# Keys and values in lasting buffers with zeroed rows, and pairs of heads taken two by two

## The chip, the cores and the metric

The kernel runs on one core of a Trainium2 chip. The metric is the device time of one execution in microseconds (us). TensorE (PE in the profile, its weight loads PEld) multiplies into the accumulation memory (PSUM), VectorE (DVE) and ScalarE (ACT) do element by element work, GpSimd (POOL) helps them, and SyncE (SP) issues most DMA transfers.

## What is computed

A linear attention over 8 batches, 8 heads, 576 positions and 64 columns, then two feed-forward layers over the 4608 rows that come out.

```python
q_s = exp(q - max(q, axis=-1)); q_s = q_s / (sum(q_s, axis=-1) + 1e-9)
k_s = exp(k - max(k, axis=2));  k_s = k_s / (sum(k_s, axis=2) + 1e-9)
kv = einsum('bhsd,bhse->bhde', k_s, v)          # 64x64 for each head
x = einsum('bhsd,bhde->bhse', q_s, kv)          # -> 4608 x 512
x = maximum(x @ w_in, 0) ** 2 @ w_out           # 512 -> 2048 -> 512
xn = x / sqrt(mean(x * x) + 1e-6) * rms_g
out = (silu(xn @ w_gate) * (xn @ w_val)) @ w_out2   # 512 -> 1536 -> 512
```

## The kernel before

The 4608 rows are taken in 9 blocks of 512 (`NB`). The first feed-forward layer runs block by block in 16 units each (`FF1`): in a unit (j, c), `p1_A` makes twelve products into `ps_h` (four 128-row pieces, three passes each over high and low halves of the numbers), ScalarE and VectorE turn them into `g` (`p1_hi`, `p1_lo`), and `p1_B` adds twelve products into `acc`, two units later. Weights come from DRAM through a ring of seven tiles `ws` (`RING`, `feed`), eight of them stay. The second layer follows from block 8 on in an order of its own (`plan2`).

Attention of block j is worked out while block j-1 is in the first layer, for blocks 0 and 1 ahead of everything (`ROUND`, lines 1150 to 1172). It goes by pairs of heads hp (four of them, `NP`), so that a pair fills 128 columns. From block 2 on each step of a pair has a place in `HALVES` (lines 1084 to 1088), counted in half units, slots: `attention(2 * i)` runs after the ps_h products of unit i, `attention(2 * i + 1)` at its end, after the acc products. Pairs are eight slots apart, line 1093 sets the start. The order of instructions on each engine is that of the program (`pinned`, `InOrder`), so a step that waits holds what is behind it on its engine.

The steps of one pair: `a_loadk`, `a_loadq`, `a_loadv` load; `a_kmax` (VectorE: `mk`), `a_kt` (TensorE transposes it into `ps_kt`), `a_mc` (VectorE: `mc`, `mcb`) and `a_kb` (TensorE: `ps_kb`) find the greatest key of each column; `a_ksub` (VectorE) and `a_kexp` (ScalarE, into `ke`) make the exponentials; `a_qmax`, `a_qsub`, `a_qexp`, `a_qsum`, `a_qn` make those of q, and `a_qT` (four transposes into `ps_q`), `a_qT_hi`, `a_qT_lo` turn them. `a_kv` multiplies `ke` by `vt` into `ps_kv`: the 576 positions are five chunks, four of 128 rows and one of 64 (`SR`), for two heads, whose results lie in the partitions 0 to 63 and 64 to 127. `vt` has a 65th column of ones, which gives the sum of the keys. Each of these products is two instructions in the trace, so a pair has 20. `a_kvf` divides (VectorE), `a_kvd_hi` and `a_kvd_lo` split the result into high and low halves, `a_x` (TensorE: `ps_x`) multiplies by q, and `a_x_hi`, `a_x_lo` (ScalarE, VectorE) write the layer's input `x`.

All steps from block 2 on that need PSUM share two banks, `a0` and `a1`, which `a_ps` hands out in turn (lines 105 to 107); a step that takes a bank waits for the last reader of the step two before it.

Beside that, `tick` converts weights (`d_load` to `d_lo`, tiles `raw`, `s`, `n`, `t`) on all three engines; from block 2 on it comes in about 11 of 20 units, and `d_out` splits the results (`so`) on ScalarE and GpSimd. At the third unit of a block `p1_out` moves the block's `acc` to `e` and to DRAM.

`a_tile` (line 394) hands out the working tiles of a pair; `A_BUFS` has how many buffers each name has in the lasting pool and, for blocks 0 and 1, more in a pool that is closed later.

Of the kernel before, what the change touches and what calls it, by code (L numbers as in the profile page):

```python
# [8 lines left out]
F32 = mybir.dt.float32  # L9
F32R = mybir.dt.float32r  # L10
# [3 lines left out]
AF = mybir.ActivationFunctionType  # L14
ALU = mybir.AluOpType
# [25 lines left out]
def attention_moe_kernel(  # L41
# [14 lines left out]
    ve, se, ge, te = (  # L56
        InOrder(tc, engine, pinned) for engine in (nc.vector, nc.scalar, nc.gpsimd, nc.tensor)
    )
    B, H, S, D = q.shape
    NT, DM = out.shape  # L60
    P = 128
# [4 lines left out]
    NP = H // 2  # L66
    FF1 = w_in.shape[0]
    FF2 = w_out2.shape[0]
    SF = S // P
    SR = S - SF * P  # L70
    OFF = S - T

    const = ctx.enter_context(tc.tile_pool(name="const", bufs=1))
# [11 lines left out]
    eps_sb = const.tile([P, 1], F32, name="eps_sb")  # L85
    g_sb = const.tile([P, KD], F32, name="g_sb")
    kvd = [
        [const.tile([P, 2, P], F32R, name=f"kvd{i}_{hp}") for hp in range(NP)] for i in range(2)
    ]
    mask = const.tile([P, 2, D], F32, name="mask")  # L90
    x2d = [tc.dram_tile([P, KD, T], F32, name=f"x2d{j}") for j in range(NB)]
# [2 lines left out]
    def held(j, ins):  # L94
        return tc.keep_in_program_order(ins) if j > 0 and not pinned[0] else ins
# [9 lines left out]
    def a_ps(j, hp, name):  # L105
        turns["a"] += 1
        return ps_a.tile([P, 512], F32, tag=f"a{turns['a'] % 2}", name=name)

    def mm3(ps, lhsT, rhs, first, last, j=0, part=False):
        for n, (a, b) in enumerate(PASSES):  # L110
            ins = te.matmul(
                ps,
                lhsT(a),
                rhs(b),
                start=first and n == 0,
                stop=last and n == 2,
                skip_group_check=part,
            )
            if n == 0:
                held(j, ins)  # L120
# [56 lines left out]
    pools = {}  # L177
# [210 lines left out]
    kts, kes, vts, qts, qns, mks, mcs, qTs, qms, kvs = ({} for _ in range(10))  # L388
    xts = {}


    A_BUFS = {"kt": (3, 1), "qt": (3, 1), "vt": (2, 2), "qn": (2, 0), "ke": (1, 1), "qT": (1, 0)}

    def a_tile(j, hp, shape, tag, dtype=F32):

        n, more = A_BUFS[tag]
        at = (j * NP + hp) % (n + more) if j < 2 else 0
        if at < n:
            return pools["a"].tile([P, *shape], dtype, tag=tag, name=tag, bufs=n)
        return pools["s"].tile([P, *shape], dtype, tag=f"{tag}{at}", name=f"{tag}s", bufs=1)  # L400
# [4 lines left out]
    def hs_(hp):  # L405
        return slice(2 * hp, 2 * hp + 2)

    def a_loadk(j, hp):
        if j >= B:
            return  # L410
        kt = kts[j, hp] = a_tile(j, hp, [2, SF + 1, D], "kt")
        if j < 2:
            nc.sync.dma_start(
                out=s_chunks(kt),
                in_=k[j, hs_(hp), 0 : SF * P, :].rearrange("h (p c) d -> p c h d", c=SF),
            )
            return
        nc.sync.dma_start(
            out=kt[:, :, 0:SF, :],
            in_=k[j, hs_(hp), 0 : SF * P, :].rearrange("h (p c) d -> p h c d", c=SF),  # L420
        )
        nc.sync.dma_start(
            out=kt[0:SR, :, SF, :], in_=k[j, hs_(hp), SF * P : S, :].rearrange("h p d -> p h d")
        )

    def a_loadq(j, hp):
# [12 lines left out]
            )  # L439
        qts[j, hp] = qt  # L440

    def a_loadv(j, hp):
        if j >= B:
            return
        hs = slice(2 * hp, 2 * hp + 2)
        vt = a_tile(j, hp, [SF + 1, 2, D + 1], "vt")
        ge.memset(vt[:, :, :, D : D + 1], 1.0)
        for h in range(2):
            nc.sync.dma_start(
                out=vt[:, 0:SF, h, 0:D],  # L450
                in_=v[j, 2 * hp + h, 0 : SF * P, :].rearrange("(p c) d -> p c d", c=SF),
            )
        nc.sync.dma_start(
            out=vt[0:SR, SF, :, 0:D], in_=v[j, hs, SF * P : S, :].rearrange("h p d -> p h d")
        )
        vts[j, hp] = vt
# [61 lines left out]
    def a_kexp(j, hp):  # L518
        if j >= B:
            return  # L520
        kt = kts.pop((j, hp))
        ke = a_tile(j, hp, [SF + 1, 2, D], "ke")
        kv_ = kt.rearrange("p h c d -> p c h d")
        for rows, cs in k_parts:
            ins = se.activation(out=ke[rows, cs], in_=kv_[rows, cs], func=AF.Exp)
            held(j, ins)
        kes[j, hp] = ke
# [48 lines left out]
    def split_hi(parts, key, dst):  # L576
        src = parts[key]
        se.activation(out=dst[:, 0], in_=src, func=AF.Copy)
        parts[key] = dst, src
# [12 lines left out]
    def a_kv(j, hp):  # L592
        if j >= B:
            return
        ps = a_ps(j, hp, "ps_kv") if j > 1 else kvs.pop((j, hp))
        ke, vt = kes.pop((j, hp)), vts.pop((j, hp))
        for c in range(SF + 1):
            m = P if c < SF else SR
            for h in range(2):
                ins = te.matmul(  # L600
                    ps[h * D : (h + 1) * D, 0 : D + 1],
                    ke[0:m, c, h, :],
                    vt[0:m, c, h, :],
                    start=c == 0,
                    stop=c == SF,
                )
                if c == 0 and h == 0:
                    held(j, ins)
        kvs[j, hp] = ps

    def a_kvd_hi(j, hp):
        if j < B:
            split_hi(kvs, (j, hp), kvd[j % 2][hp])

    def a_kvd_lo(j, hp):
        if j < B:
# [3 lines left out]
    def a_kvf(j, hp):  # L620
        if j >= B:
            return
        ps = kvs.pop((j, hp))
        rk = pools["a"].tile([P, 1], F32, tag="rk", name="rk")
        ve.tensor_scalar_add(out=rk, in0=ps[:, D : D + 1], scalar1=1e-9)
        ve.reciprocal(out=rk, in_=rk)

        if j < 2:
            f = pools["sk"[j]].tile([P, P], F32, tag=f"kvf{hp}", name="kvf", bufs=1)
        else:  # L630
            f = pools["a"].tile([P, P], F32, tag="kvf", name="kvf")
        ve.scalar_tensor_tensor(
            out=f.rearrange("p (h d) -> p h d", h=2),
            in0=ps[:, 0:D].unsqueeze(1).to_broadcast([P, 2, D]),
            scalar=rk,
            in1=mask,
            op0=ALU.mult,
            op1=ALU.mult,
        )
        kvs[j, hp] = f  # L640
# [10 lines left out]
    def s_chunks(kt):  # L651
        t = kt.rearrange("p h c d -> p (h c d)")[:, 0 : 2 * SF * D]
        return t.rearrange("p (c h d) -> p c h d", c=SF, h=2)
# [52 lines left out]
        te.transpose(ps[0:SR, P : 2 * P], ek[:, SF * P : S], ident)  # L706

    def s_kc(j, hp):
        ke = kes[j, hp] = a_tile(j, hp, [SF + 1, 2, D], "ke")
        se.activation(  # L710
            out=ke[:, 0:SF].rearrange("p c h d -> p (c h d)"), in_=kT.pop((j, hp)), func=AF.Copy
        )
        ve.tensor_copy(
            out=ke[0:SR, SF].rearrange("p h d -> p (h d)"), in_=kvs[j, hp][0:SR, P : 2 * P]
        )
# [33 lines left out]
    def a_x(j, hp):  # L749
        ps = a_ps(j, hp, "ps_x")  # L750
        qT = qTs.pop((j, hp))
        p0 = min(j * OFF // NG, P)
        view = ps.rearrange("p (c t) -> p c t", c=NG)
        for b, lo, hi in ((j - 1, 0, p0), (j, p0, P)):
            if lo == hi:
                continue
            t = kvd[b % 2][hp]
            mm3(
                view[:, :, lo:hi],
                lambda a: t[:, a, :],  # L760
                lambda a: qT[:, a, :].rearrange("p (c t) -> p c t", c=NG)[:, :, lo:hi],
                True,
                True,
                j,
            )
        xts[j, hp] = ps
# [314 lines left out]
        return min(NJ1 + 4 + len(at) * 11 // 20, len(jobs) + 4)  # L1081


    HALVES = ((-12, a_loadk), (-10, a_loadq), (-3, a_kmax), (-2, a_qmax), (0, a_qsub))
    HALVES += ((0, a_loadv), (2, a_qexp), (3, a_kt), (3, a_qsum), (4, a_mc), (4, a_qn))
    HALVES += ((6, a_kb), (7, a_ksub), (8, a_kexp), (8, a_qT), (9, a_qT_hi), (10, a_qT_lo))
    HALVES += ((10, a_kv), (11, a_kvf), (12, a_kvd_hi), (13, a_kvd_lo), (14, a_x))
    HALVES += ((15, a_x_hi), (16, a_x_lo))
    todo = {}
    for j in range(2, NB):  # L1090
        for hp in range(NP):
            for n, (at, f) in enumerate(HALVES):
                at += (j - 1) * 2 * FF1 - (9 if j == 2 else 11) + 2 * FF1 // NP * hp
                todo.setdefault(at, []).append((-n, j, hp, f))
    for l in todo.values():
        l.sort(key=lambda x: x[:3])
# [19 lines left out]
    with ExitStack() as ctx_a:  # L1116
# [8 lines left out]
        def at_(f, r):  # L1125
            if 0 <= r < len(heads):
                f(*heads[r])

        a_loadk(0, 0)
        make_identity(nc, ident)  # L1130
        ge.tensor_scalar(
            out=neg_r, in0=ident, scalar1=-1.0, scalar2=0.0, op0=ALU.mult, op1=ALU.add
# [98 lines left out]
        for i, (j, c) in enumerate(units):  # L1231
# [54 lines left out]
            s = i - (n1 - FF1)  # L1286
# [6 lines left out]
        at = 0  # L1293
        for op in plan2:
# [4 lines left out]
            else:  # L1299
                _, s, n, q = op  # L1300
# [49 lines left out]
```

## Time and profile before

| | us |
|---|---|
| median of three runs | 1737.18 |
| lowest and highest run | 1733.74, 1738.27 |
| profiled execution, its time | 1733.5 |
| profiled execution, its span | 1731.5 |
| TensorE busy, matmuls | 1707.3 |
| VectorE busy | 1059.1 |
| ScalarE busy | 763.4 |

The span is the time from the first to the last instruction that the profile shows. Matmuls overlap in the records (one of 512 columns is shown with 0.39 us, though the next starts sooner), so what a group costs is read from the starts. A group on the timeline is a run of like instructions, and x20 is how many. All attention work of blocks 2 to 8 lies between about 130 and 760 us.

### The profile page before, as it was taken

To read this page: it belongs to the slowest core of one execution; us is meant where nothing else is said; L and a number is where in the kernel's file an instruction comes from. 1 tells how busy PE (TensorE), PEld (TensorE's weight loads), DVE (VectorE), ACT (ScalarE), POOL (GpSimd) and SP (SyncE) were. 2 spreads that over 40 slices of the span, in tenths; PEclk is the share of its full clock that TensorE was granted. 3 is DMA by queue.
4 is the path that set the end of the run, shared out by engine and by line. 5 is a ranking of instruction groups with operands and counts; after the bars stand their busy time and mean duration, and the time that the engine had idled before them with its cause. 6 is when DMAs were issued, how large, how long until landed. Compare 5 with 4: busy or idle time off the path is not lost.

```text
span 1731.5 us, 23049 instructions
## 1 busy us (share of the span) xinstructions
PE 1707.3 (99%) x8390; PEld 1410.3 (81%) x8390; DVE 1059.1 (61%) x1847; ACT 763.4 (44%) x1336; POOL 151.8 (9%) x167
## 2 busy tenths in 40 slices
PE   6999999999999999999999999999999999999998
PEld 5788888788888878888888888888888888888997
DVE  7996555565565556431566787757765776646344
ACT  6875445545555554443544325332523243223122
POOL 2000001223333223220000000000000000000000
PEclk9999999999999999999999999999999999999999
DMA  9986657788888877576465557566756666665885
GB/s 213 317 285 246 201 174 229 227 292 278 275 281 258 285 246 248 177 254 208 158 204 196 195 191 268 186 219 194 267 192 211 196 232 203 219 192 193 289 304 202
DMA packets 190560, 398.42 MB, mean 230 GB/s; under 512 B 65520, under 2 KB 102384, under 8 KB 189296
## 3 DMA queue, kind: packets, MB, share of 16 engines
q1 hardware_dynamic: 162416, 356.05, 64.0%
q10 hardware_dynamic: 28032, 40.90, 6.7%
q8 instruction: 67, 1.10, 0.3%
q14 instruction: 45, 0.37, 0.1%
HBM read 337.12 MB, written 59.77 MB: 229 GB/s over the span
## 4 chain that ended last, share of the span: by engine, by line
PE 95%; DVE 2%; ACT 1%; SPq 0%; DMA 0%; issue 0%; POOL 0%; DVEq 0%; POOLq 0%; ACTq 0%
PE acc L34 39%; PE ps_h L34 22%; PE ps_x L34 10%; PE ps_y L34 9%; PE ps_v L34 8%; PE ps_w L34 4%; PE ps_kv L34 1%; DVE t L34 1%; PE ps_q L34 1%; PE ps_kb L34 0%; PE ps_kt L34 0%; DVE qs L34 0%; PE ps_s L34 0%; DMA qt<-in_q 0%; DMA vt<-in_v 0%
## 5 line engine op out<-in xcount | busy, mean ns | idle before, releaser
L34 PE MATMUL ps_h<-x,ws 128*128 128x512 f32 x1296 | 316.6, 394 | 0.7 <-ACT r L34 0.7
L34 PE MATMUL acc<-ws,g 128*128 128x512 f32 x1296 | 313.4, 390 | 1.0 <-ACT g L34 0.9
L34 PE MATMUL acc<-g,ws 128*128 128x512 f32 x1296 | 313.8, 391 | 0.0
L34 PEld LDWEIGHTS acc<-ws,g 128*128 128x128 f32 x1296 | 241.4, 188 | 51.3 <-ACT g L34 2.1
L34 PEld LDWEIGHTS acc<-g,ws 128*128 128x128 f32 x1296 | 241.7, 188 | 50.9
L34 PEld LDWEIGHTS ps_h<-x,ws 128*128 128x128 f32 x1296 | 239.6, 188 | 50.8 <-ACT r L34 1.5
L34 ACT ACTIVATE g<-r 128x512 fp32r<-128x512 f32 x252 | 159.1, 631 | 230.5 <-DVE r L34 225.4
L34 DVE TENSOR_TENSOR g<-r,g 128x512 fp32r<-128x512 f32 x252 | 172.6, 685 | 116.9 <-ACT g L34 115.2
L34 ACT ACTIVATE r<-ps_h 128x512 f32<-128x512 f32 x144 | 85.7, 595 | 232.7 <-PE ps_h L34 232.6
L34 PE MATMUL ps_y<-xo,ws 128*128 128x512 f32 (+1 forms) x720 | 168.6, 369 | 0.0
L34 PE MATMUL ps_v<-xo,ws 128*128 128x512 f32 (+1 forms) x720 | 168.4, 368 | 0.0
L34 PE MATMUL ps_x<-xo,ws 128*128 128x512 f32 (+1 forms) x720 | 167.4, 368 | 0.0
L34 PEld LDWEIGHTS ps_x<-xo,ws 128*128 128x128 f32 x720 | 128.0, 188 | 23.5
L34 PEld LDWEIGHTS ps_v<-xo,ws 128*128 128x128 f32 x720 | 127.7, 188 | 23.4
L34 PEld LDWEIGHTS ps_y<-xo,ws 128*128 128x128 f32 x720 | 126.4, 189 | 24.2 <-DVE sa L34 1.5
L34 PE MATMUL ps_h<-x,w 128*128 128x512 f32 x432 | 106.1, 395 | 0.0
L34 PE MATMUL acc<-g,w 128*128 128x512 f32 x432 | 104.4, 391 | 0.0
L34 PEld LDWEIGHTS acc<-g,w 128*128 128x128 f32 x432 | 80.7, 188 | 16.9
L34 PEld LDWEIGHTS ps_h<-x,w 128*128 128x128 f32 x432 | 79.7, 188 | 17.0 <-issue 0.4
L34 ACT ACTIVATE r<-r 128x512 f32<-128x512 f32 x144 | 91.0, 632 | 4.5
L34 DVE TENSOR_TENSOR u<-ps_y,p 128x512 f32<-128x512 f32 (+1 forms) x120 | 76.0, 633 | 22.9 <-PE ps_y L34 21.5
L34 ACT ACTIVATE sg<-silu 128x512 f32<-128x512 f32 (+1 forms) x90 | 51.5, 585 | 82.4 <-DVE silu L34 82.3
(138 smaller groups left out, 1823.4 us busy)
## 6 DMA issues: line engine op xcount, KB each, us to landing
ws<-wd_t SPq DMA_DIRECT2D x210, 512.0 KB, 4.2
ws<-wd_u SPq DMA_DIRECT2D x108, 512.0 KB, 4.2
ws<-wd_o SPq DMA_DIRECT2D x96, 512.0 KB, 4.4
ws<-wd_i SPq DMA_DIRECT2D x89, 512.0 KB, 4.4
wd_t<-so ACTq DMA_DIRECT2D x84, 256.0 KB, 4.7
raw<-in_w_out SPq DMA_DIRECT2D x28, 512.0 KB, 5.2
raw<-in_w_gv SPq DMA_DIRECT2D x24, 512.0 KB, 5.6
x2d<-e SPq DMA_DIRECT2D x36, 256.0 KB, 3.0
```

Source lines behind the costliest of these rows:

```text
L34: ins = f(*args, **kw)
```

## The change

- Keys (`ke`) and values (`vt`) of blocks get lasting buffers (`kbuf`, `vbuf`), made once at the start by `a_bufs`: rows 64 to 127 of the fifth chunk are set to zero and the column of ones to one, by GpSimd. Loads and exponentials never write those rows again. The memset at each load of v is gone.
- `a_kv` uses all 128 rows in the fifth chunk too.
- From block 2 on two pairs of heads share a plan of 16 slots: `FIRST` for the even pair, `SECOND` for the odd one. `a_kv` of both stands in slot 9 and writes two halves of one PSUM bank; `a_kvf2`, `a_kvd2_hi` and `a_kvd2_lo` then work on both. The start is 4 slots ahead of the block's instead of 11 (9 for block 2).
- `kvd` tiles hold two pairs each; `kt` and `qt` have two buffers in the lasting pool instead of three.

```diff
-        [const.tile([P, 2, P], F32R, name=f"kvd{i}_{hp}") for hp in range(NP)] for i in range(2)
+        [const.tile([P, 2, 2, P], F32R, name=f"kvd{i}_{n}") for n in range(NP // 2)]
+        for i in range(2)
...
-    A_BUFS = {"kt": (3, 1), "qt": (3, 1), "vt": (2, 2), "qn": (2, 0), "ke": (1, 1), "qT": (1, 0)}
+    A_BUFS = {"kt": (2, 2), "qt": (2, 2), "qn": (2, 0), "qT": (1, 0)}
...
+    kbuf, vbuf = [], []
+
+    def a_bufs(pool, n, bufs, name, shape):
+
+        for at in range(n):
+            t = pool.tile([P, *shape], F32, tag=f"{name}{len(bufs)}", name=name, bufs=1)
+            ge.memset(t[SR:P, SF], 0.0)
+            if shape[-1] > D:
+                ge.memset(t[:, :, :, D : D + 1], 1.0)
+            bufs.append(t)
...
-        vt = a_tile(j, hp, [SF + 1, 2, D + 1], "vt")
-        ge.memset(vt[:, :, :, D : D + 1], 1.0)
+        vt = vbuf[(j * NP + hp) % (4 if j < 2 else 2)]
...
-        ke = a_tile(j, hp, [SF + 1, 2, D], "ke")
+        ke = kbuf[hp % 2]
...
-        ps = a_ps(j, hp, "ps_kv") if j > 1 else kvs.pop((j, hp))
+        if j < 2:
+            ps, o = kvs.pop((j, hp)), 0
+        else:
+            if hp % 2 == 0:
+                kvs[j, hp // 2] = a_ps(j, hp, "ps_kv")
+            ps, o = kvs[j, hp // 2], hp % 2 * P
...
-            m = P if c < SF else SR
             for h in range(2):
                 ins = te.matmul(
-                    ps[h * D : (h + 1) * D, 0 : D + 1],
-                    ke[0:m, c, h, :],
-                    vt[0:m, c, h, :],
+                    ps[h * D : (h + 1) * D, o : o + D + 1],
+                    ke[:, c, h, :],
+                    vt[:, c, h, :],
...
+    def a_kvf2(j, hp):
...
+        ps = kvs.pop((j, hp // 2))[:, 0 : 2 * P].rearrange("p (n d) -> p n d", n=2)
+        rk = pools["a"].tile([P, 2], F32, tag="rk", name="rk")
+        ve.tensor_scalar_add(out=rk, in0=ps[:, :, D], scalar1=1e-9)
+        ve.reciprocal(out=rk, in_=rk)
+        f = pools["a"].tile([P, 2, P], F32, tag="kvf", name="kvf", bufs=1)
+        for n in range(2):
+            ve.scalar_tensor_tensor(
...
-    HALVES = ((-12, a_loadk), (-10, a_loadq), (-3, a_kmax), (-2, a_qmax), (0, a_qsub))
-    HALVES += ((0, a_loadv), (2, a_qexp), (3, a_kt), (3, a_qsum), (4, a_mc), (4, a_qn))
-    HALVES += ((6, a_kb), (7, a_ksub), (8, a_kexp), (8, a_qT), (9, a_qT_hi), (10, a_qT_lo))
-    HALVES += ((10, a_kv), (11, a_kvf), (12, a_kvd_hi), (13, a_kvd_lo), (14, a_x))
-    HALVES += ((15, a_x_hi), (16, a_x_lo))
+    FIRST = ((-9, a_loadk), (-6, a_loadq), (-4, a_loadv), (0, a_kmax), (1, a_kt), (2, a_mc))
+    FIRST += ((4, a_kb), (4, a_qmax), (5, a_ksub), (5, a_qsub), (6, a_kexp), (7, a_qexp))
+    FIRST += ((8, a_qsum), (9, a_qn), (9, a_kv), (11, a_qT), (12, a_qT_hi), (13, a_qT_lo))
+    FIRST += ((14, a_x), (15, a_x_hi), (16, a_x_lo))
+    SECOND = ((-7, a_loadk), (-3, a_loadq), (-2, a_loadv), (3, a_kmax), (4, a_kt), (5, a_mc))
+    SECOND += ((6, a_kb), (7, a_qmax), (7, a_ksub), (8, a_kexp), (8, a_qsub), (9, a_qexp))
+    SECOND += ((9, a_kv), (10, a_kvf2), (11, a_qsum), (11, a_kvd2_hi), (12, a_qn))
+    SECOND += ((12, a_kvd2_lo), (13, a_qT), (15, a_qT_hi), (16, a_qT_lo), (17, a_x))
+    SECOND += ((18, a_x_hi), (19, a_x_lo))
...
-            for n, (at, f) in enumerate(HALVES):
-                at += (j - 1) * 2 * FF1 - (9 if j == 2 else 11) + 2 * FF1 // NP * hp
+            for n, (at, f) in enumerate(SECOND if hp % 2 else FIRST):
+                at += (j - 1) * 2 * FF1 - 4 + 4 * FF1 // NP * (hp // 2)
...
         a_loadk(0, 0)
+        for pool, n, bufs, name in (("a", 2, kbuf, "ke"), ("a", 2, vbuf, "vt"), ("s", 2, vbuf, "vt")):
+            a_bufs(pools[pool], n, bufs, name, [SF + 1, 2, D + (name == "vt")])
```

## Rows read from the trace of the kernel before

**Rows 1.** The page, part 1: busy us, share of the span, instructions.

```profile
PE 1707.3 (99%) x8390; PEld 1410.3 (81%) x8390; DVE 1059.1 (61%) x1847; ACT 763.4 (44%) x1336; POOL 151.8 (9%) x167
```

**Rows 2.** Busy by stretch; columns: stretch, length, engines, clock, DMA share, GB/s.

```profile
0.00:60.00 60.00, 46.07 (x349) 33.30 (x350) 49.21 (x119) 41.04 (x78) 10.39 (x30) 1.00 0.90 225
...
340.00:750.00 410.00, 405.29 (x2095) 332.18 (x2095) 235.62 (x445) 212.23 (x379) 117.63 (x109) 1.00 0.81 261
```

**Rows 3.** TensorE's waits from 130 to 900 us; columns: total us, times, longest us.

```profile
PE ps_q L34 <- DVE x L34: 4.6, 2, 3.2
```

**Rows 4.** Timeline of TensorE at one visit of products; columns: start, length (us), what.

```profile
453.19 0.39 PE L34 MATMUL acc<-g,w 128*128 128x512 f32 x1
...
453.51 0.95 PE L34 MATMUL ps_kv<-vt,ke 128*64 128x65 f32 x20
...
453.68 0.40 PE L34 MATMUL ps_kv<-vt,ke 128*64 128x65 f32 x8
...
453.91 0.29 PE L34 MATMUL ps_kv<-vt,ke 128*64 128x65 f32 x4
...
454.13 0.33 PE L34 MATMUL ps_kv<-vt,ke 64*64 64x65 f32 x4
...
454.39 0.50 PE L34 MATMUL ps_h<-x,ws 128*128 128x512 f32 x1
...
454.73 0.39 PE L34 MATMUL ps_h<-x,ws 128*128 128x512 f32 x1
```

**Rows 5.** The same timeline: ordinary products of the feed-forward layer, and four transposes.

```profile
447.98 2.88 PE L34 MATMUL acc<-g,ws 128*128 128x512 f32 x12
...
450.70 1.52 PE L34 MATMUL acc<-g,w 128*128 128x512 f32 x6
...
444.80 0.60 PE L34 MATMUL ps_q<-ident,qn 128*128 128x128 f32 x4
...
445.48 0.39 PE L34 MATMUL ps_h<-x,ws 128*128 128x512 f32 x1
```

**Rows 6.** VectorE by line, 340 to 660 us: busy us, mean ns, idle before.

```profile
L34 DVE TENSOR_REDUCE mk<-kt 128x128 f32<-128x512 f32 x13 | 14.2, 1093 | 0.0
...
L34 DVE TENSOR_TENSOR mk<-mk,kt 64x128 f32<-64x128 f32 x13 | 4.7, 362 | 0.4
...
L34 DVE TENSOR_REDUCE mc<-ps_kt 128x1 f32<-128x128 f32 x13 | 3.7, 285 | 0.7
...
L34 DVE COPY mcb<-mc 128x128 f32<-128x128 f32 x13 | 3.7, 286 | 0.4
...
L34 DVE TENSOR_TENSOR g<-r,g 128x512 fp32r<-128x512 f32 x52 | 35.0, 674 | 10.5 <-ACT g L34 10.5
...
L34 DVE TENSOR_TENSOR x<-ps_x,x 128x512 fp32r<-128x512 f32 x13 | 8.8, 679 | 0.0
...
L34 DVE SCALAR_TENSOR_TENSOR t<-s,t 128x512 uint32<-128x512 uint32 x25 | 22.5, 900 | 0.9
...
L34 DVE CUSTOM_DVE_ANT_0 t<-t,n 128x1024 uint16<-128x1024 uint16 x25 | 19.3, 771 | 0.9
...
L34 DVE TENSOR_SCALAR t<-s 128x512 uint32<-128x512 uint32 x26 | 11.9, 458 | 1.5 <-POOL so L34 1.5
```

**Rows 7.** Timeline before TensorE's longest wait; VectorE's waits (130 to 800 us).

```profile
343.16 1.70 DVE L34 SCALAR_TENSOR_TENSOR t<-s,t 128x512 uint32<-128x512 uint32 x1
...
344.89 1.64 DVE L34 CUSTOM_DVE_ANT_0 t<-t,n 128x1024 uint16<-128x1024 uint16 x1
...
347.28 0.63 PE L34 MATMUL ps_q<-ident,qn 128*128 128x128 f32 x4 [3.25 <-DVE x L34]
...
DVE t L34 <- POOL so L34: 5.0, 2, 3.6
```

**Rows 8.** Timeline: the first product; page, part 6: a ring load, us to landing.

```profile
5.36 0.66 PE L34 MATMUL ps_l<-ident,kl 64*128 64x64 f32 x4 [5.36 <-DMA kl<-in_k]
...
ws<-wd_i SPq DMA_DIRECT2D x89, 512.0 KB, 4.4
```

More of the change, by code (lines that the diff above doesn't have):

```diff
@@ L608, in a_kv, with a_kvd2_hi, a_kvd2_lo @@
                     held(j, ins)
-        kvs[j, hp] = ps
+        if j < 2:
+            kvs[j, hp] = ps
+    def a_kvf2(j, hp):
+        if j >= B:
+            return
+        ps = kvs.pop((j, hp // 2))[:, 0 : 2 * P].rearrange("p (n d) -> p n d", n=2)
[5 more added lines that the diff above has]
+            ve.scalar_tensor_tensor(
+                out=f[:, n].rearrange("p (h d) -> p h d", h=2),
+                in0=ps[:, n, 0:D].unsqueeze(1).to_broadcast([P, 2, D]),
+                scalar=rk[:, n : n + 1],
+                in1=mask,
+                op0=ALU.mult,
+                op1=ALU.mult,
+            )
+        kvs[j, hp // 2] = f
+    def a_kvd2_hi(j, hp):
+        if j < B:
+            t = kvd[j % 2][hp // 2]
+            se.activation(out=t[:, :, 0], in_=kvs[j, hp // 2], func=AF.Copy)
+    def a_kvd2_lo(j, hp):
+        if j < B:
+            t = kvd[j % 2][hp // 2]
+            ve.tensor_tensor(
+                out=t[:, :, 1],
+                in0=kvs.pop((j, hp // 2)),
+                in1=t[:, :, 0].bitcast(F32),
+                op=ALU.subtract,
+            )
     def a_kvd_hi(j, hp):
         if j < B:
-            split_hi(kvs, (j, hp), kvd[j % 2][hp])
+            split_hi(kvs, (j, hp), kvd[j % 2][hp // 2][:, hp % 2])
     def a_kvd_lo(j, hp):
@@ L623, in a_kvf @@
         ps = kvs.pop((j, hp))
-        rk = pools["a"].tile([P, 1], F32, tag="rk", name="rk")
+        rk = pools["a"].tile([P, 2], F32, tag="rk", name="rk")[:, 0:1]
         ve.tensor_scalar_add(out=rk, in0=ps[:, D : D + 1], scalar1=1e-9)
         ve.reciprocal(out=rk, in_=rk)
[L628 to L631, printed above, removed]
+        f = pools["sk"[j]].tile([P, P], F32, tag=f"kvf{hp}", name="kvf", bufs=1)
         ve.scalar_tensor_tensor(
@@ L708, in s_kc @@
     def s_kc(j, hp):
-        ke = kes[j, hp] = a_tile(j, hp, [SF + 1, 2, D], "ke")
+        ke = kes[j, hp] = kbuf[hp % 2]
         se.activation(
@@ L756, in a_x @@
                 continue
-            t = kvd[b % 2][hp]
+            t = kvd[b % 2][hp // 2][:, hp % 2]
             mm3(
```

## The prediction

> **What bounds the kernel now.** I read the page's first part, then the busy times by stretch, then TensorE's own waits, and last its timeline at single visits. TensorE is busy 99% of the span [rows 1]. After the first 60 us, where it is idle 14 us and VectorE is busy 49, it hardly stops: between 340 and 750 us it lacks 4.7 us of 410 [rows 2], and nearly all of that is one kind of wait, the transposes of q waiting for VectorE's x [rows 3]. So a microsecond less of work on TensorE's queue is a microsecond less of time, and other engines count only where TensorE waits for them. VectorE is at 57% there.
>
> A feed-forward product of 512 columns starts every 0.227 us (twelve from 447.98 to 450.70) [rows 5]. Four transposes put between two such products take 0.68 us from the first transpose to the second product after them, less one ordinary spacing 0.45, or 0.11 each [rows 5]: going from one type of work to another is free as long as both use all 128 rows and columns of the array. The visit of one pair of heads' ps_kv products, with 64 columns, is different. The product before it starts at 453.19, ps_kv at 453.51, the next feed-forward product at 454.39 and the one after that at 454.73 [rows 4]. That is 1.54 us, less two ordinary spacings 1.09 us for one visit.
>
> **What the visit consists of** [rows 4]. Five chunks of 128, 128, 128, 128 and 64 rows. From chunk 2 to chunk 4 there are 0.23 us, so 0.115 a chunk. Chunk 1 takes 0.17, so 0.055 more; the wait ahead of it is 0.32 instead of 0.227, so 0.09 more. From chunk 4 to the short one there are 0.22, 0.105 too many, and the short chunk up to the next product takes 0.26, and then the next spacing is 0.34, 0.11 too many. The reading that fits all of it: each change of the tile's shape (128x128 to 128x64, 128x64 to 64x64, 64x64 to 128x128) costs some 0.15 to 0.2 us, and there are three in a visit.
>
> **Part 1, the full-row short chunk.** It takes out the change from 128x64 to 64x64: the 0.105 and the 0.055 that chunk 5 pays on entering, 0.16 a visit. There are 24 visits in the blocks 2 to 7 (six blocks, four pairs of heads): 3.8 us. Twice the rows cost nothing where columns set the pace, as chunks 2 to 4 show. Blocks 0 and 1 have 8 more visits, at most 1.3 us, in the first 60 us, where VectorE's chain sets the pace as much as TensorE; from 0 to 1.3 I take 0.5.
>
> **Part 2, two visits in one.** In the new order both pairs' ps_kv come in the same slot with nothing of TensorE between them, into one PSUM bank. The last chunk's 0.26 less the 0.055 of its own entry is 0.205, 0.09 more than a chunk. So one entry (0.09 + 0.055) and one exit (0.09 + 0.11) are saved for two pairs: 0.345, 12 times: 4.1 us. Together, from the rows: two visits 2.17; the new double one 0.32 + 0.17 + 8 x 0.115 + 0.205 + 0.34 less 0.453, so 1.50. The difference, 0.67, carries the rounding of eight starts; with the parts above (2 x 0.16 + 0.345) it is 0.665, and from the starts to the nanosecond 0.64. I take 0.65, 12 times: 7.8 us. Bounds: 4 (one of the two parts alone) to 8.
>
> **Part 3, TensorE's waits.** A slot is half a unit: after the twelve ps_h products or after the twelve acc products; they are numbered here from the first pair's kmax, which is 0. Today the q transposes take the PSUM bank that x of the pair before held, and x_lo stands in the very slot of those transposes, behind a unit's conversion of weights on VectorE. At 347.28 TensorE had waited 3.25 us for it [rows 7]; 4.6 us in all [rows 3]. In the new order, written out with the alternation of the two banks, the transposes of q take banks whose readers are done well before: the first pair's (slot 11) that of the second ps_kb, read in slot 7; the second pair's (slot 13) that of ps_kv, read in slot 10. So these 4.6 us go, unless something new is late.
>
> What is late next? Every step now stands one to three slots behind what it needs. The tightest I find is ps_kt of the second pair in slot 4: VectorE can take mc of the first pair only when its ps_kt is out (slot 1), and has then to do mc (0.285 + 0.286), the low half of g (0.674), perhaps one conversion (0.458 + 0.900 + 0.771 = 2.13), x_lo of the pair before (0.679) and kmax (1.093 + 0.362): 3.4 us, or 5.5 with the conversion [rows 6]. TensorE in that time does three groups of twelve, 36 x 0.227 = 8.2 us. Some 2.7 us to spare, and the conversion comes in 11 units of 20 only. At slower conversions (0.41 + 1.70 + 1.64, as before the longest wait [rows 7]) it is 7.1, still in time. I take no new wait; the other end stands with the rivals.
>
> **What else moves, at nothing.** GpSimd loses the memset at each load of v (it had to wait for the last reader of its buffer) and gets ten small ones at the start; the first product waits there for a DMA until 5.36 us [rows 8], so they lie behind that wait. Loads of k, q and v go to other slots, and k and q have two buffers instead of three. SyncE issues them in order, ahead of ring loads, so a late release would hold those up. But k's buffer is asked for one slot after its exponential is issued, q's one slot after its last reader, v's three or more; and a ring load lands in 4.4 us [rows 8] with seven tiles in the ring, each lasting a group of twelve products, 2.7 us: 19 us less 4.4, so some five slots of delay are covered; past that the ring would run dry. All loads of two pairs now lie in eight of sixteen slots, with the DMA engines at 0.81 on average [rows 2]; they have nine slots or more before use. VectorE does kvf and the low half of kvd of two pairs in five instructions instead of eight, which is off the path. In block 2's steps nothing ends later than before; in later blocks the last x_lo comes two slots later, one ahead of the first product of the next block, whose tenth product needs it 2 us after.
>
> **Sum.** 7.8 + 4.6 + 0.5 = 12.9 us. The profiled execution took 1733.5 us (its span 1731.5); 1720.6 for it. It was the quickest of those shown; their median is 1737.2, so 3.7 more: 1724.3.
>
> **Rivals.**
> (a) The waits come back in another place, about as many as now: the steps stand closer, and VectorE waits for GpSimd too, 3.6 us once [rows 7]. For it: one-slot distances everywhere; against: the sum of 5.5 against 8.2. Then 7.8 + 0.5 are left: 1729.
> (b) Padding is worth nothing: the gap ahead of the short chunk is not of the shape but of the ends of its accumulation. Then 1724 + 3.8 = 1728. In its favour, from the Trainium skill (TensorE: Matmul & The Clock Gate, "Why this matters for your kernels"): a product of fewer rows lasts as long as one of 128, and short rows gain by running beside others, which this change gives up. No run here shows the two side by side; chunk 5's late start in [rows 4] speaks against it, and so does another page of the skill (TensorEngine Tiling, "Tiling Modes"), by which a change of the tiling mode empties the array.
> (c) Both at once: only the merging's 4.1 is left: 1733, no change that can be told.
> (d) Slower. VectorE misses the second ps_kt. With a slowed conversion and a 3.6 us wait for GpSimd [rows 7] ahead of it, the chain is 7.1 + 3.6 = 10.7 against 8.2: 2.5 us late. If that were so in all twelve double visits, 30 us would be added to the forecast: 1754. It decides from 12.9 / 12, or 1.1 us of lateness in each on. Against it: two such waits for GpSimd in all of 130 to 800 us. The Trainium skill (SBUF — State Buffer, "SBUF: two separate sides") gives the mechanism: VectorE with two SBUF inputs and GpSimd exclude each other for a whole instruction. The trace has 1.70 against a mean of 0.90 for one such instruction.
>
> **Chances.** Forecast 0.47; (a) 0.22; (b) 0.08; (c) 0.11; (d) 0.12. A change below 0.3%, 5.2 us, can't be told from none. Forecast, (a) and (b) are faster by more: 0.77; (c) within: 0.11; (d) slower: 0.12. The range runs from 1716 (8 for the visits, 4.6 and 1.3 make 13.9 below the profiled 1733.5, so 1720, and 4 of scatter, the distance of that run from the median) to 1735 (over (c) and its scatter); (d) and scatter are left out, about 0.2.
>
> **What would show it.** After: ps_kv in groups of 40 records with 128 rows throughout, 1.3 us from the first start to the next product and no gap between chunk 4 and 5; twelve such groups after block 1; TensorE's waits for VectorE gone between 130 and 900 us. Wrong would be: a gap at the fifth chunk with 128 rows too (b), a gap or another product between the two pairs, ps_kt, ps_kb or ps_x waiting for VectorE (a, d), or ps_h or acc waiting for a ring load.

## The result, and the profile after

The changed kernel takes 1722.85 us (median of four runs, 1722.04 to 1723.12) against 1737.06 (four runs, 1733.74 to 1738.27); the ratio is 0.992, with a 95% interval of 0.9909 to 0.9932. It is faster by 14.2 us. The profiled executions are 10.4 us apart (1733.5 and 1723.12, spans 1731.5 and 1721.3); where the other 3.8 us come from is told below.

Part 1 of the page and the busy times by stretch, of the changed kernel, answering to [rows 1] and [rows 2]:

```profile
PE 1699.7 (99%) x8390; PEld 1409.3 (82%) x8390; DVE 1064.4 (62%) x1811; ACT 758.0 (44%) x1324; POOL 151.2 (9%) x145
```

```profile
0.00:60.00 60.00, 44.44 (x343) 32.05 (x344) 47.57 (x116) 39.63 (x75) 11.30 (x31) 0.97 0.89 217
...
340.00:750.00 410.00, 410.00 (x2156) 339.64 (x2156) 243.71 (x431) 212.74 (x377) 120.26 (x97) 1.00 0.82 269
```

TensorE is busy 7.6 us less, and in the stretch from 340 to 750 us it has no idle time left (4.7 us before). The start is no shorter in this execution: TensorE's granted clock was 0.97 in the first 60 us (1.00 in the execution of [rows 2]), and the first ps_h product came 1.5 us later than there.

TensorE's waits from 130 to 900 us (total us, times, longest), answering to [rows 3]:

```profile
PE ps_kt L34 <- DVE mk L34: 0.4, 1, 0.4
```

The waits of the q transposes are gone. What stays is one of another kind: the first ps_kt of block 2 waits 0.4 us for kmax, at 153 us.

The timeline of one double visit (start us, length us, what), answering to [rows 4]. Rows cut out of a group at a later moment begin with the oldest product still running, and carry the shape of that one though the group may hold others:

```profile
488.20 0.39 PE L34 MATMUL acc<-g,w 128*128 128x512 f32 x1
...
488.52 1.39 PE L34 MATMUL ps_kv<-vt,ke 128*64 128x65 f32 x40
...
488.92 0.41 PE L34 MATMUL ps_kv<-vt,ke 128*64 128x65 f32 x8
...
489.04 0.40 PE L34 MATMUL ps_kv<-vt,ke 128*64 128x65 f32 x8
...
489.15 0.41 PE L34 MATMUL ps_kv<-vt,ke 128*64 128x65 f32 x8
...
489.83 0.50 PE L34 MATMUL ps_h<-x,ws 128*128 128x512 f32 x1
...
490.17 0.39 PE L34 MATMUL ps_h<-x,ws 128*128 128x512 f32 x1
```

All 40 products have 128 rows. The fourth chunk starts at 488.92, the fifth at 489.04, the first of the second pair at 489.15: 0.12 and 0.11 apart, with no gap ahead of the fifth chunk and none between the pairs. From the last acc product to the second ps_h product there are 490.17 - 488.20 = 1.97 us, less two ordinary spacings 1.52 for two pairs of heads, where two visits took 2.17. All twelve double visits of the trace take 1.52.

VectorE's waits for GpSimd from 130 to 800 us, 1.5 us where there were 5.0, answering to the last of [rows 7], and the first product, 0.25 us later than in [rows 8]:

```profile
DVE t L34 <- POOL so L34: 1.5, 1, 1.5
```

```profile
5.61 0.66 PE L34 MATMUL ps_l<-ident,kl 64*128 64x64 f32 x4 [5.61 <-DMA kl<-in_k]
```

### The profile page after: what moved, and what is told of

It is laid out like the page before. It is cut to its first block, busy times and chain, and to the rows that moved or that the text cites. A ratio compares the mean times of both kernels' runs of the same rounds, so it can differ in the third digit from the quotient of the medians.

```text
span 1721.3 us, 22968 instructions
## 1 busy us (share of the span) xinstructions
PE 1699.7 (99%) x8390; PEld 1409.3 (82%) x8390; DVE 1064.4 (62%) x1811; ACT 758.0 (44%) x1324; POOL 151.2 (9%) x145
## 4 chain that ended last, share of the span: by engine, by line
PE 95%; DVE 2%; ACT 1%; DMA 1%; issue 0%; SPq 0%; POOL 0%; DVEq 0%; POOLq 0%
PE acc L34 39%; PE ps_h L34 22%; PE ps_x L34 10%; PE ps_y L34 9%; PE ps_v L34 9%; PE ps_w L34 4%; PE ps_kv L34 1%; DVE t L34 1%; PE ps_q L34 1%; DMA qt<-in_q 0%; DMA raw<-in_w_in 0%; PE ps_kb L34 0%; PE ps_kt L34 0%; PE ps_s L34 0%; DVE qs L34 0%
## 5 line engine op out<-in xcount | busy, mean ns | idle before, releaser
L34 DVE TENSOR_TENSOR g<-r,g 128x512 fp32r<-128x512 f32 x252 | 177.2, 703 | 131.3 <-ACT g L34 129.6
```

What stands on the lines that cost most here:

```text
L34: ins = f(*args, **kw)
```

## The experiments

All times are medians; the kernel before ran beside each batch, with 1736.5 us (E0 to E3), 1736.7 (E4, E5, E6 and E8) and 1737.2 (E7). Some comparisons below leave out the start: they take the time of a profiled execution from its first ps_h product of the feed-forward layer to the end of its span. Those first products are:

```profile
48.61 3.27 PE L34 MATMUL ps_h<-x,w 128*128 128x512 f32 x12
49.95 3.27 PE L34 MATMUL ps_h<-x,w 128*128 128x512 f32 x12
50.10 3.26 PE L34 MATMUL ps_h<-x,w 128*128 128x512 f32 x12
48.94 3.27 PE L34 MATMUL ps_h<-x,w 128*128 128x512 f32 x12
49.91 3.27 PE L34 MATMUL ps_h<-x,w 128*128 128x512 f32 x12
48.10 3.26 PE L34 MATMUL ps_h<-x,w 128*128 128x512 f32 x12
```

in this order those of the kernel before, E0, the changed kernel, E3, E4 and E7. From there to the end (the spans are 1731.5, 1734.1, 1721.3, 1724.0, 1728.4 and 1720.5) there are 1682.9, 1684.1, 1671.2, 1675.1, 1678.5 and 1672.4 us.

| kernel | us | runs | ratio to before (95%) |
|---|---|---|---|
| before, once more (E0) | 1736.0 | 1 | |
| E1 before, full rows | 1731.8 | 7 | 0.9966 to 0.9989 |
| E2 changed, 64 rows | 1728.2 | 4 | 0.9939 to 0.9968 |
| E3 changed, visits apart | 1726.1 | 4 | 0.9927 to 0.9957 |
| E4 changed, 64 rows and apart | 1730.2 | 4 | 0.9948 to 0.9978 |
| E5 before, q transposes later | 1732.8 | 10 | 0.9974 to 0.9992 |
| E6 before, short chunk third | 1741.4 | 9 | 1.0015 to 1.0036 |
| E7 changed, two reductions more | 1723.4 | 4 | 0.9910 to 0.9943 |
| E8 changed, four reductions more | 1743.0 | 1 | |

### E0: the kernel before, once more

> The kernel of before once more, for what one execution differs from another in the first 60 us and in TensorE's waits for VectorE. Theory: the three waits of the q transposes come from the order of the program, so they come again with about 4.6 us in all, and the first ps_h product starts within 0.5 us of 48.6. Rival: both change by more than that from execution to execution, and then 1 to 2 us of the difference to the changed kernel are chance.

TensorE's waits from 130 to 900 us in that execution:

```profile
PE ps_q L34 <- DVE x L34: 4.7, 3, 3.2
```

The wait of 3.2 us comes again, and 4.7 us in all: it belongs to the order of the program. The start does not hold still: the first ps_h product came at 49.95 us, not within 0.5 of 48.6. So the start alone moves an execution by more than a microsecond. Another 1.2 us of the distance to the first execution came between 50 and 130 us, where ps_h waited 1.9 us for ScalarE's r in place of 0.7.

### E1: full rows alone

```diff
-        vt = a_tile(j, hp, [SF + 1, 2, D + 1], "vt")
-        ge.memset(vt[:, :, :, D : D + 1], 1.0)
+        vt = vbuf[(j * NP + hp) % (4 if j < 2 else 2)]
...
-            m = P if c < SF else SR
...
-                    ke[0:m, c, h, :],
-                    vt[0:m, c, h, :],
+                    ke[:, c, h, :],
+                    vt[:, c, h, :],
```

> The kernel of before with the lasting buffers and the full-row fifth chunk alone; order of the pairs as before, one buffer of keys from block 2 on. Theory (a change of the tile's shape costs 0.16 us): a visit takes 0.93 instead of 1.09 us, 24 visits give 3.8 us, the waits of the q transposes stay near 4.6: 1733 against 1737. Rival (the gap ahead of the short chunk belongs to the end of the accumulation): visits stay at 1.09 and the time at 1737.

Measured: 1731.8, 4.7 us less than before in the same batch, with an interval of 0.11 to 0.34%, or 1.9 to 5.9 us. TensorE's waits are the same three (3.2, 0.2 and 1.3 us), so the buffers and the rows alone leave them as they were. Padding is worth something; how much exactly this pair of medians doesn't tell. The trace does: the visit at 453 us takes 0.93 us, as expected, 0.16 less than in [rows 4].

### E2: the changed kernel with 64 rows

```diff
-                    ke[:, c, h, :],
-                    vt[:, c, h, :],
+                    ke[0 : P if c < SF else SR, c, h, :],
+                    vt[0 : P if c < SF else SR, c, h, :],
```

> The changed kernel with 64 rows in the fifth chunk again (buffers, order and double visits stay). Theory (each change of shape costs): in each of the 12 double visits three changes come back, two of 0.16 into 64x64 and one of 0.15 from the first pair's 64x64 back to 128x64, so 0.47 a double visit, 5.6 us, and up to 1.3 at the start: 1728.5 to 1730 against 1722.9. Rival (end of accumulation): 1723, no change. A third: only the two entries count, 3.8: 1726.7.

Measured: 1728.2, 5.4 us more than the changed kernel, 0.3 under the lower end. The timeline of one double visit:

```profile
439.86 0.39 PE L34 MATMUL ps_h<-x,ws 128*128 128x512 f32 x1
...
440.18 1.83 PE L34 MATMUL ps_kv<-vt,ke 128*64 128x65 f32 x40
...
440.80 0.33 PE L34 MATMUL ps_kv<-vt,ke 64*64 64x65 f32 x4
...
441.06 0.39 PE L34 MATMUL ps_kv<-vt,ke 128*64 128x65 f32 x6
...
441.68 0.33 PE L34 MATMUL ps_kv<-vt,ke 64*64 64x65 f32 x4
...
441.94 0.50 PE L34 MATMUL ps_h<-x,ws 128*128 128x512 f32 x1
...
442.27 0.40 PE L34 MATMUL ps_h<-x,ws 128*128 128x512 f32 x1
```

The short chunks begin at 440.80 and 441.68, and at 441.06 the second pair's first. From 439.86 to 442.27, less two spacings, there are 1.96 us instead of 1.52: 0.44 a double visit, 5.3 in twelve. So all three changes of shape cost, the way back to 128x64 too; two entries alone would have been 3.8.

### E3: the two pairs' visits apart

```diff
-    SECOND += ((9, a_kv), (10, a_kvf2), (11, a_qsum), (11, a_kvd2_hi), (12, a_qn))
-    SECOND += ((12, a_kvd2_lo), (13, a_qT), (15, a_qT_hi), (16, a_qT_lo), (17, a_x))
+    SECOND += ((10, a_kv), (11, a_kvf2), (11, a_qsum), (12, a_kvd2_hi), (12, a_qn))
+    SECOND += ((13, a_kvd2_lo), (13, a_qT), (15, a_qT_hi), (16, a_qT_lo), (17, a_x))
```

> The changed kernel with the second pair's ps_kv one slot later, so that two single visits with full rows stand in place of one double visit (kvf, the high and the low halves one slot later too). Theory: one entry and one exit come back for each, 0.345 x 12 = 4.1 us, no new wait of TensorE: 1727 against 1722.9. Rival (being together saves nothing, all of the gain of the visits is in the rows): 1723.

Measured: 1726.1, 3.2 us more than the changed kernel. In the two profiled executions the time from the first ps_h product to the end, which leaves the start out, is 1675.1 against 1671.2, so 3.9 us. The edit parts only ten of the twelve double visits. In block 2 two slots follow each other with no product between them, and two visits stay double:

```profile
171.82 1.39 PE L34 MATMUL ps_kv<-vt,ke 128*64 128x65 f32 x40
```

Ten times the 0.345 us of one entry and one exit are 3.45 us, between the two measured figures. Being together is worth what one entry and one exit cost.

### E4: the new order alone

The edits of E2 and E3 in one kernel. Here too two of the twelve double visits stay double.

> The changed kernel with 64 rows in the fifth chunk and the two pairs' ps_kv in different slots: the new order without either saving in the visits. Theory (the order takes away TensorE's waits and nothing else): visits of 1.09 us, no wait of the q transposes, 4.6 us under the kernel of before: 1732 against 1736.5 to 1737. Rival (the waits went because the visits got shorter): the waits are back in some place and the time is 1736 to 1737.

TensorE's waits from 130 to 900 us:

```profile
PE ps_kt L34 <- DVE mk L34: 0.4, 1, 0.4
```

The waits are gone though the visits are as long as before (all but the two double ones), so it is the order that took them away. The time, 1730.2, is 6.5 us under the median of before in the same batch and not 4.6; 0.4 of it are the two double visits. Without the start, the profiled executions are 1682.9 and 1678.5, 4.4 us apart, which is no more than the waits last. So what the medians show on top, some 2 us, lies in executions of the kernel before that took longer than its profiled one. The experiments now make a ladder from before to the changed kernel: order 6.5, then full rows 4.1 (E4 to E3), then together 3.2 (E3 to the changed kernel); the other way round, together at 64 rows 2.0 (E4 to E2), then full rows 5.4.

### E5: the old order with the q transposes one slot later

```diff
-    HALVES += ((6, a_kb), (7, a_ksub), (8, a_kexp), (8, a_qT), (9, a_qT_hi), (10, a_qT_lo))
+    HALVES += ((6, a_kb), (7, a_ksub), (8, a_kexp), (9, a_qT), (10, a_qT_hi), (11, a_qT_lo))
...
-                at += (j - 1) * 2 * FF1 - (9 if j == 2 else 11) + 2 * FF1 // NP * hp
+                at += (j - 1) * 2 * FF1 - 11 + 2 * FF1 // NP * hp
```

> The kernel of before with the four transposes of q and the two halves of q one slot later, so that x_lo stands a slot ahead of the transposes that need its bank (block 2 starts as the others do, 11 slots ahead). Theory (the 4.6 us are that one distance): TensorE's waits go, 1732 against 1736.5. Rival (VectorE is late anyway): the transposes or what follows wait as long in the new place, 1736.

```profile
PE ps_kt L34 <- DVE qT L34: 1.5, 1, 1.5
PE ps_q L34 <- DVE x L34: 0.6, 1, 0.6
PE ps_h L34 <- ACT r L34: 0.2, 1, 0.2
```

Measured: 1732.8, 3.9 us less. That is not the theory to the letter: the transposes' own wait shrinks from 4.7 to 0.6 us, and a new one of 1.5 us comes in block 2, where ps_kt takes the bank of the q transposes and waits for the low half of q, which stood one slot ahead of it and now stands in its very slot. (The edit also starts block 2 two slots earlier, and the wait comes in no other block.) In all 2.3 us of waits are left. Moving one step alone pushes part of the wait on to the next.

### E6: the short chunk third

```diff
-        for c in range(SF + 1):
+        for c in (0, 1, SF, 2, 3):
...
-                    stop=c == SF,
+                    stop=c == SF - 1,
```

> The kernel of before with the 64-row chunk taken third instead of last. Theory (each change of the tile's shape costs): one more change in a visit, from 64x64 back to 128x64, 0.15 us, 24 visits 3.6 us and 8 at the start up to 1.2: 1740 to 1741.5 against 1736.5, and a visit of 1.24 us. Rival (the gap belongs to the end of the accumulation, or to the last chunk whatever it is): the gap stays ahead of the last chunk and the time at 1736.5.

Measured: 1741.4, 4.7 us more. One visit:

```profile
409.57 0.39 PE L34 MATMUL acc<-g,ws 128*128 128x512 f32 x1
...
409.89 1.10 PE L34 MATMUL ps_kv<-vt,ke 128*64 128x65 f32 x20
...
410.12 0.43 PE L34 MATMUL ps_kv<-vt,ke 128*64 128x65 f32 x4
...
410.27 0.33 PE L34 MATMUL ps_kv<-vt,ke 64*64 64x65 f32 x4
...
410.54 0.39 PE L34 MATMUL ps_kv<-vt,ke 128*64 128x65 f32 x6
...
410.92 0.50 PE L34 MATMUL ps_h<-x,ws 128*128 128x512 f32 x1
...
411.26 0.40 PE L34 MATMUL ps_h<-x,ws 128*128 128x512 f32 x1
```

The gap goes along with the shape: two products of 64x64 start at 410.27, 0.15 after the last of 128x64 ahead of them at 410.12 (the ordinary distance is 0.058, half of a chunk's 0.115), and the next 128x64 at 410.54; the last chunk is now a full one and has no gap ahead. The visit takes 411.26 - 409.57 - 0.45 = 1.24 us, as expected. That the gap belongs to the end of the accumulation is refuted. What this isolates is the change of rows, 128x64 to 64x64 and back. For the way in from 128x128 and out to it no run separates the change of columns from the short products themselves (65 columns behind 512).

The same execution shows how a wait of TensorE can cost more than it lasts. Its timeline after the long wait of the q transposes; the group behind the same wait in the kernel before; and the busy times by stretch of E6 (stretch, length, PE, PEld, DVE, ACT, POOL, granted clock, DMA share, GB/s):

```profile
350.48 0.71 PE L34 MATMUL ps_q<-ident,qn 128*128 128x128 f32 x4 [3.24 <-DVE x L34]
...
350.87 4.59 PE L34 MATMUL ps_h<-x,ws 128*128 128x512 f32 x12
...
355.29 2.89 PE L34 MATMUL acc<-g,ws 128*128 128x512 f32 x12
```

```profile
347.66 2.98 PE L34 MATMUL ps_h<-x,ws 128*128 128x512 f32 x12
```

```profile
340.00:346.00 6.00, 6.00 (x32) 5.08 (x31) 2.87 (x6) 4.43 (x9) 0.00 (x0) 1.00 0.31 105
...
352.00:355.00 3.00, 3.00 (x10) 2.38 (x9) 0.55 (x1) 0.63 (x1) 0.00 (x0) 0.61 0.88 308
...
355.00:360.00 5.00, 5.00 (x23) 4.13 (x23) 0.00 (x0) 2.94 (x5) 1.29 (x1) 1.00 0.41 145
```

After 3.2 us of idling the granted clock is 0.61 between 352 and 355 us, where it was 1.00 before and is again after 355: part of that stretch runs at 1.2 GHz instead of 2.4. The twelve ps_h products last 4.59 us on the timeline, not the 2.98 of the group behind the same wait in the kernel before, where the clock stayed at 1.00: 1.6 us more, on top of the wait.

### E7 and E8: how much room the tightest place has

Two (E7) and four (E8) reductions more of 1.09 us ahead of `mk` of the second pair, between the ps_kt of the first pair and that of the second; the result is the same. The edit of E8, which was made first:

```diff
+        for _ in range(4 * (hp % 2)):
+            ve.tensor_reduce(
+                out=mk, in_=kt[:, :, 0:SF].rearrange("p h c d -> p h d c"), axis=AX.X, op=ALU.max
+            )
         ve.tensor_reduce(
             out=mk, in_=kt[:, :, 0:SF].rearrange("p h c d -> p h d c"), axis=AX.X, op=ALU.max
```

> The changed kernel with four more reductions of 1.09 us ahead of kmax of the second pair (same result): 4.4 us more work for VectorE between ps_kt of the first pair and ps_kt of the second. Theory (the sum: 3.4 us of work, 5.5 with a conversion, against 8.2): 7.8 without and 9.9 with a conversion, so about half of the twelve places wait 1.7 us each, 10 us, and the time is near 1733. Rival (VectorE is far ahead at that place and the distance is larger): no wait, 1723. Other rival (it is closer than the sum): all twelve wait 3 us or more, 1760.

With four, TensorE's waits from 130 to 900 us, and the timeline around one of them:

```profile
PE ps_kt L34 <- DVE mk L34: 15.8, 10, 2.1
```

```profile
381.66 2.89 PE L34 MATMUL ps_h<-x,ws 128*128 128x512 f32 x12
...
386.75 0.33 PE L34 MATMUL ps_kt<-ident,mk 128*128 128x128 f32 x1 [2.09 <-DVE mk L34]
...
386.85 4.53 PE L34 MATMUL acc<-g,ws 128*128 128x512 f32 x12
```

It is the predicted place, ps_kt for `mk`. Nine of the twelve double visits wait, not half of them; the longest are 2.1 us, not 1.7. That adds 15.4 us, and the time, 1743.0, lies 20 above the changed kernel, twice what was expected. Part of the rest stands in the last line: the acc group after the wait lasts 4.53 us instead of 2.88, the slower clock again, this time after 2.1 us of idling (the granted clock is 0.53 from 388.4 to 391.5 us). The trace has it after two of the nine waits, some 3.3 us in all; where the other 1.4 us lie stays open.

> The changed kernel with two more reductions of 1.09 us at the same place (four made TensorE wait ten times, 2.05 us at most of them). Theory (with a conversion in between the place has 8.2 - 5.5, by the four reductions 4.4 - 2.05, so 2.3 to 2.7 us to spare): 2.2 us more fit, no new wait over 0.1 us beside the 0.4 of the changed kernel itself, and the time stays within 1 us of 1722.9. Rival (the waits of the kernel with four come from VectorE's total load and not from this one distance): they shrink in proportion, some ten waits of 1 us, 1732.

```profile
PE ps_kt L34 <- DVE mk L34: 0.8, 2, 0.4
```

With two, one wait of 0.4 us is added, which the expectation had not, and the time is 1723.4. So 2.2 us more all but fit and 4.4 don't. At the place of that wait there are 2.2 - 0.4 = 1.8 us to spare by E7 and 4.4 - 2.1 = 2.3 by E8.

The start of E7 is that of the changed kernel, since the reductions come from block 2 on only. In this execution its first 60 us ran at the full clock:

```profile
0.00:60.00 60.00, 45.08 (x351) 32.82 (x352) 49.34 (x119) 41.44 (x79) 11.30 (x31) 1.00 0.90 227
```

## Why the prediction was right

The forecast was 1724.3 with a range of 1716 to 1735, and 1722.85 came. The mechanisms hold for the visits and the waits. That the total came within 1.5 us is partly luck: the profiled execution was forecast 2.5 us too low and the way from it to the median 4 us too long.

- **The full-row chunk (3.8 us).** Confirmed: E4 to E3 gives 4.1, E1 gives 4.7 with a wide interval and 0.16 a visit in its trace, and E6 shows that the gap follows the shape. That twice the rows cost nothing could not be read from chunks 2 to 4, which all have 128 rows; the changed kernel shows it, where the full fifth chunk takes 0.11 us like the others. Rival (b), that padding is worth nothing, falls, and (c) with it. The rule of the Trainium skill that stood behind it (TensorE: Matmul & The Clock Gate, "Why this matters for your kernels") is not refuted for a product by itself, but it doesn't reckon a visit, since it leaves out the change of shape. The other rule (the Trainium skill, TensorEngine Tiling, "Tiling Modes"), by which a change of mode empties the array, agrees with E6's 0.15 us.
- **Two visits in one (4.1 us).** Confirmed for the ten of twelve that E3 parts: 3.45 by the prediction's price, 3.2 from the medians of E3 and the changed kernel, 3.9 without the start. The double visit was put at 1.50 us and takes 1.52.
- **TensorE's waits (4.6 us).** They went, and E4 shows that the order did it. In the profiled executions they cost about what they last (4.4 us from before to E4 without the start, with 0.4 of it from the two double visits). Between medians this term was mis-sized: E4 has 6.5 us, 1.9 more. E6 and E8 show what can be added, products at the slower clock after a long wait; in E6 that is 1.6 us for one wait. That the same lies behind the 1.9 us is argued, see below.
- **What is late next (nothing).** Right except for 0.4 us at the first ps_kt of block 2, whose kmax stands one slot before it in block 0's crowded units; I had looked at the steady order only. The sum for the tightest place, 2.7 us to spare with a conversion, was 0.4 to 0.9 too high (2.3 by E8, 1.8 by E7). Rivals (a) and (d) didn't happen, but (d)'s late ps_kt is a real danger: E8 makes it happen with 4.4 us more work. GpSimd's part in (d) was not tried.
- **The start (0.5 us).** Neither shown nor refuted. The first ps_h product came at 50.1 us against 48.6 in the profiled executions, but the granted clock of the first 60 us was 0.97 against 1.00. E0, at 0.97 too, has 49.95. E7, whose start is that of the changed kernel, had the full clock there and 48.10, 0.5 earlier than before. These are single executions, and what moves the start from one to the next is larger than the term.
- **From the profiled execution to the median (3.7 us).** I took the distance between the two for the kernel's own scatter and added it after the change too. After the change it is gone: the profiled execution took 1723.12, the median is 1722.85. Between profiled executions the change is 10.4 us where 12.9 were forecast (12 times 0.65 or 7.8 for the visits and 4.6 less 0.4 for the waits, less 1.5 at the start, make 10.5); between medians it is 14.2. The forecast of the median came out because the later start and the vanished distance have opposite signs. The vanished distance and the 1.9 us of the waits are in the main the same microseconds, seen once from the profiled execution and once from E4.

Why the distance went is in part argued. Eighteen runs of the kernel before lie in order of their mean granted clock: 1733.8 us at 1.000, 1734.7 to 1735.2 at 0.999, 1736.0 to 1736.6 at 0.998, 1736.8 to 1738.7 at 0.997 and 0.996. The changed kernel's four lie at 0.998 and 0.999, 1.1 us apart. So most executions of the kernel before had more time at the slower clock than its profiled one. That this lay after the wait of the q transposes is shown for E6, which has the same wait, and not for the kernel before itself: in neither of its two profiled executions did the clock fall there. The start is a rival: in E1's profiled execution, at a mean of 0.998, the lower clock lies in the first 60 us alone (0.94 there). A mean does not tell which.

## What to carry to other kernels

On a TensorE that is never idle, look for places where the tile's shape changes: each change cost some 0.15 to 0.2 us here, so bring products of one shape together and fill short chunks with zeros to the full rows, if the zeros can be written once. When steps are written into a fixed order, put one slot between a step and the reader that frees its PSUM bank; with the distance at none, three of the 28 sets of q transposes waited, up to 3.2 us. And allow for a wait of TensorE to cost more than its length: behind one of 3.2 us and two of 2.1 us here the next group lasted 1.6 us longer, behind the others it did not.

## What the runs showed of the hardware

- Going from products of 128x128 to those of 128x64, or from 128x64 to 64x64, and back cost 0.15 to 0.2 us each (E6 and E2 isolate the change between 128x64 and 64x64, at 0.15), while full-array transposes between products cost nothing beyond their own 0.11 us [rows 5].
- The granted clock can fall after waits of TensorE of 2.1 and 3.2 us in the middle of dense work. It doesn't in every execution: the same 3.2 us wait was followed by the full clock in the profiled executions of before, E0 and E1 and by 0.61 in E6, and of the nine waits of E8 (0.75 to 2.1 us) two of 2.1 us were followed by a lower clock. It made the next group of twelve 1.6 us longer.
